# Folding q's shift row onto 64 partitions, and Wo with the masked sums split into high and low parts

## The chip, the cores and the metric

The kernel runs on one core of a Trainium2 chip. The metric is the device time of one execution in microseconds; the number for the kernel before is the median of three runs. Engines are named as in the profile: PE is TensorE's matmul stream (PEld its weight loads), DVE is VectorE, ACT is ScalarE, POOL is GpSimd, SP is SyncE, which only issues DMAs here.

## The reference

One block on a sequence of S = 2048 tokens with D = 448 channels, in float32. Six modulation rows of D numbers come from `silu(c) @ w_mod`. A linear-attention block and a token-mixing MLP follow, each with a layer norm, a scale and a shift ahead of it and a gate behind it:

```python
sa, ca, ga, sb, cb, gb = six rows of silu(c) @ w_mod
h = layernorm(x) * (1 + ca) + sa
q, k, v = split(h @ wqkv)              # 16 heads of 28
pq, pk = phi(q), phi(k)                # phi(t) = where(t > 0, t + 1, exp(t)) + 1e-6
kv = pk^T v per head;  z = sum of pk over the tokens
o = (pq kv) / (pq z + 1e-6)
x = x + ga * (o @ wo)
h = layernorm(x) * (1 + cb) + sb
x = x + gb * (gelu(h^T w1 + b1) w2 + b2)^T      # over the token axis, F = 1792
```

## The kernel before

The tokens are 16 tiles of 128. The order of the work is written out by hand: each engine does its instructions in the order in which the program text issues them, and what a helper issues lands at that place in the queues of all engines that it uses. A wait on one engine therefore holds up all that stands behind it there.

**Number formats.** A float32 matmul (`F32` operands) shows in the trace as two instructions, one of `F32R` operands as one. Most products are made as three `F32R` matmuls from a high and a low part of each operand. `split(full, hi, lo)` (line 82) makes the parts: a copy on ACT rounds to `hi`, a subtraction on DVE leaves `lo`.

**First stage: k, the sums and the first q.** The layer norm is folded into the projections. The scale `1 + ca` is multiplied into the weights (`w_high`, `w_low`); what the mean subtracts and what the shift `sa` adds come as a few extra rows of the moving operand, `Wrow[j]`, against matching rows of the tile of x (j = 0 for q, 1 for k). Those rows are made so: `row_part` (line 275) sums the raw weights times `sa` over the four chunks on DVE into `accb[j]`, 128 partitions by 448; `row_sum` (283) puts seven F32R matmuls with the selector `sel_s` into the bank `rowb[j]`; `row_bias` (289) ends the sum with one float32 matmul of `sel_b` and `accb[j]`; `row_out` (292) copies the rows into `Wrow[j]` with ACT and takes their low part with DVE. `close(t, j)` (437) is the last matmul of a projection and reads `Wrow[j]`.

The loop `for t in range(4, NT)` (682) issues, in each turn, the k projection of tile t+1 (`project`, line 684), `close(t, 1)`, at t=9 `row_sum(0)` and `row_bias(0)`, then the outer products of tile t-4 with its keys (`a_outer`, 545, into the four banks `cacc`), every second turn the transposition of statistics rows (`a_transpose`, 401), and from t=10 an early q projection (`a_q`, 476). The work of ACT and DVE comes after that in the text of the same turn: exponentials (`a_exp`), copies of the transposed rows (`a_copy`), splits of x (`a_split_high`, `a_split_low`), key parts (`a_pk_parts`, 517, the low part by an accumulating DMA from POOL's queue, line 528), the normed x and its parts (`a_norm`, `a_high`, `a_low`), at the end of t=9 `row_out(0)` (751), one step a turn of a modulation sum (`mod_part`, 227), and from t=13 Wo times the gate `ga` (779).

**Between the stages.** The last outer products, the key sum `zp`, two q projections, then `kvb` (818), the keys' products with v's weights in float32; `kvm` (822) is `kvb` times a mask that keeps the blocks of the heads. After one more q projection, four float32 matmuls (968) of `kvm` and the gated Wo make `wp`, 112 rows at a time; ACT copies them (970), DMAs lay them out in chunks of 128 rows (977), and `wp_split` (980) makes their high and low parts. `split_to` (319) splits pieces of w1 in the meantime, `load_to` loads them.

**Second stage.** For each tile a turn of the loop at 988: normalise the q side (`b_prod`, `b_sum`, `b_eps`, `b_recip`, `b_scale`), transpose, multiply by `wp`, add to x, second layer norm, and from turn 5 on the first product of the MLP. The rest of the MLP follows from line 1293 on, w2's products from 1319 on.

Of the kernel before, what the change touches and what calls it, by code (L numbers as in the profile page):

```python
# [8 lines left out]
F32 = mybir.dt.float32  # L9
# [5 lines left out]
P = 128  # L15
# [36 lines left out]
def block_kernel(ctx: ExitStack, tc: tile.TileContext, x, xt, wqkv, wo, w1, b1, w2, c, wmod, wfirst, out):  # L52
# [50 lines left out]
    cst.tile([P, 112], F32, name="space")  # L103
# [12 lines left out]
    sel_s = cst.tile([P, ROWS], F32R, name="sel_s")  # L116
    rowst = []
# [171 lines left out]
    def row_bias(j):  # L289
        nc.tensor.matmul(rowb[j][:ROWS, :D], sel_b, accb.pop(j), start=False, stop=True)  # L290
# [226 lines left out]
    def a_pk_parts(t):  # L517
        if t not in pks:
            a_pk_high(t)
        a_pk_low(t)  # L520
# [159 lines left out]
    wo_sb = []  # L680
    late = [t for t in range(NT) if t not in Q_EARLY.values()]
    for t in range(4, NT):
        if 5 < t < NT - 1:
            project(t + 1, 1, "kp")
        kp = close(t, 1) if t > 4 else kps[4]
        if t == 9:
            row_sum(0)
            row_bias(0)
# [28 lines left out]
        a_pk_parts(t - 1)  # L717
        highs = HIGH_AT.get(t, (t - 2,))
# [5 lines left out]
        if t == 11:  # L724
            low2 = mod_high(2)
# [24 lines left out]
        if t == 9:  # L750
            row_out(0)
# [8 lines left out]
        if t == 10:  # L760
            mod_add(2)
# [16 lines left out]
        if t >= 13:  # L778
            nc.vector.tensor_mul(wo_sb[t - 13], wo_sb[t - 13], mods[2][:G])
        load_to(PRE_LOAD.get(t, 0))  # L780


    a_pk_parts(NT - 1)
    nc.vector.tensor_add(pksum[1], pksum[1], pksum[0])
    zs = (moving(slot, "zh"), moving(slot, "zl"))
    split(pksum[1], *zs)
    load_to(10)
    a_phi_q()
    a_outer(NT - 4)
    a_outer(NT - 3)  # L790
    nc.vector.tensor_mul(wo_sb[3], wo_sb[3], mods[2][:G])
    for i in (2, 3):
        mod_part(3, i)
    split_to(2)
    a_outer(NT - 2)
    a_outer(NT - 1)
    zp = bank("zp")
    for i, pk in enumerate(zs):
        nc.tensor.matmul(zp[:, :D], ones_r, pk, start=(i == 0), stop=(i == 1))
    zb = tslot("zb")  # L800
    nc.scalar.activation(zb, zp[:, :D], AF.Copy, bias=S * 1e-6)
    load_to(14)
    split_to(4)
    a_q(late.pop(0))
    csum = []
    for ch in range(4):
        csum.append(slot(f"cs{ch}"))
        nc.scalar.activation(csum[ch], cacc[ch][:, :D], AF.Identity, scale=col[1][:, ch:ch + 1])
        nc.vector.scalar_tensor_tensor(csum[ch], zb, col[0][:, ch:ch + 1], csum[ch], op0=ALU.mult, op1=ALU.add)
    a_phi_q()  # L810
    a_q(late.pop(0))
    split_to(6)
    mp = mod_sum2(4)
    kvb = bank("kvb")
    for ch in range(4):
        for g in range(4):
            s = slice(g * G, (g + 1) * G)
            nc.tensor.matmul(kvb[:G, s], raw_w[2, ch][:, s], csum[ch][:, s], start=(ch == 0 and g == 0),  # L818
                             stop=(ch == 3), skip_group_check=True)
    a_phi_q()  # L820
    kvm = slot("kvm", parts=G)
    nc.vector.tensor_mul(kvm, kvb[:G, :D], mask)
    mod_out(4, mp)
    load_to(PRE + MID + 3)
    split_to(8)
    Wpr, Wph, Wpl = [], [], []


    H2h, H2l = [None] * NT, [None] * NT
    pns, phs, ys, opb, sums, nms, nm2s, rss, vss = {}, {}, {}, {}, {}, {}, {}, {}, {}  # L830

# [16 lines left out]
    def b_scale(t):  # L848
# [6 lines left out]
        pq[t] = None  # L855

# [106 lines left out]
    for fn in (b_prod, b_sum, b_eps, b_recip, b_scale):  # L963
        fn(0)
    mod_add(3)
    for g in range(4):
        wp = bank(f"wp{g}")
        nc.tensor.matmul(wp[:G, :D], kvm[:, g * G:(g + 1) * G], wo_sb[g], start=True, stop=True)  # L968
# [19 lines left out]
    for i in range(NT + LAG):  # L988
# [72 lines left out]
        if i == 0:  # L1061
            for ch in range(4):
                wp_split(ch)
# [323 lines left out]
```

## Time and profile before

| | |
|---|---|
| time, median of 3 runs (lowest to highest) | 433.37 us (433.33 to 433.41) |
| the profiled execution's own time | 434.09 us |
| its span, first to last instruction | 432.4 us |
| instructions | 7216 |
| DMA | 66.14 MB, mean 153 GB/s |

The page gives each engine's busy time in the whole span, then the chain of work that ended last, followed back from the end. The timelines list instructions with their start, their length and, in brackets, how long their engine stood idle before them and which instruction released it. A matmul's length there is that of one instruction from its start to its modelled end; matmuls overlap, so what one costs in a stream is the distance between the starts of two, or the length of a row of the chain over its count (`x11` is eleven instructions). The start of a row of the chain can be some tenths of a microsecond behind that of its first instruction in the timeline, since the chain gives the overlap to the earlier one. The table by windows gives, after the busy times, the granted clock, the busy share of the DMA engines (1 is full) and GB/s.

### The profile page before, as it was taken

What the parts mean: (1) busy time and instruction counts of PE and PEld (TensorE: products, weight loads), DVE (VectorE), ACT (ScalarE), POOL (GpSimd) and SP (SyncE); (2) the same over time, 40 slices, a digit from 0 to 9 for tenths busy, and PEclk for the clock granted to TensorE, in tenths of its full rate; (3) what the DMA queues carried; (4) which work ended last, traced back from release to release, by engine and by line L of the source; (5) the groups of instructions that cost most, each with busy time, mean ns of one, the idle gap of its engine ahead of it and who ended that gap; (6) DMA issues with size and microseconds to landing.
All of it is one profiled execution on the core that took longest, in us unless ns stands there. A gap on an engine that the chain in (4) does not pass through costs nothing.

```text
span 432.4 us, 7216 instructions
## 1 busy us (share of the span) xinstructions
PE 427.9 (99%) x2331; PEld 398.0 (92%) x2331; DVE 365.1 (84%) x814; ACT 278.9 (65%) x595; POOL 120.1 (28%) x199
## 2 busy tenths in 40 slices
PE   8999999999999999999999999999999999999997
PEld 8888899999899999999999999999999999999996
DVE  4899987889899999998579695739799998898894
ACT  5799869658578899996755263537464664655550
POOL 4345444300026577775200000010113131132010
PEclk9999999999999999999999999999999999999999
DMA  8997997565300036354427461577379977986431
GB/s 282 385 337 162 239 264 162 89 206 193 86 1 0 26 74 148 74 125 97 145 85 244 142 212 50 166 203 210 79 193 214 207 159 159 214 170 144 85 46 41
DMA packets 63797, 66.14 MB, mean 153 GB/s; under 512 B 4816, under 2 KB 55312, under 8 KB 63760
## 3 DMA queue, kind: packets, MB, share of 16 engines
q1 hardware_dynamic: 54688, 50.90, 37.8%
q0 software_dynamic: 8784, 14.32, 20.8%
q10 hardware_dynamic: 288, 0.46, 0.4%
q8 instruction: 18, 0.29, 0.3%
q14 instruction: 19, 0.16, 0.1%
HBM read 46.30 MB, written 7.34 MB: 124 GB/s over the span
## 4 chain that ended last, share of the span: by engine, by line
PE 97%; DVE 1%; ACT 1%; issue 0%
PE y L1183 19%; PE up L951 10%; PE up L950 10%; PE up L952 10%; PE y L1184 9%; PE cacc L554 7%; PE qp L432 7%; PE op L893 7%; PE kp L432 6%; PE op L900 1%; PE warm L188 1%; PE tq L863 1%; PE qp L439 1%; PE kvb L818 1%; PE wp L968 1%; PE rowb L287 1%
## 5 line engine op out<-in xcount | busy, mean ns | idle before, releaser
L950 PE MATMUL up<-h2h,ph 128*128 128x448 f32 x224 | 81.2, 362 | 0.0
L951 PE MATMUL up<-h2l,ph 128*128 128x448 f32 x224 | 81.2, 362 | 0.0
L952 PE MATMUL up<-h2h,pl 128*128 128x448 f32 x224 | 80.8, 361 | 0.0
L1138 POOL DMA_DIRECT2D a<-a x16 | 14.2, 964 | 142.6 <-DMA pr<-in_B_w_dram 76.7
L950 PEld LDWEIGHTS up<-h2h,ph 128*128 128x128 f32 x224 | 42.0, 188 | 3.1
L952 PEld LDWEIGHTS up<-h2h,pl 128*128 128x128 f32 x224 | 41.9, 187 | 3.0
L951 PEld LDWEIGHTS up<-h2l,ph 128*128 128x128 f32 x224 | 42.0, 188 | 2.3
L84 DVE TENSOR_TENSOR pl<-pr,ph 128x512 fp32r<-128x512 f32 x46 | 30.7, 688 | 2.6 <-ACT ph L83 1.7
L1189 ACT ACTIVATE cc<-y 128x448 f32<-128x448 f32 x24 | 13.0, 546 | 26.7 <-PE y L1184 26.7
L1102 DVE TENSOR_TENSOR u<-u,mod 128x448 f32<-128x448 f32 x14 | 8.7, 623 | 23.0 <-ACT u L1101 22.8
L83 ACT ACTIVATE ph<-pr 128x512 fp32r<-128x512 f32 x46 | 27.6, 623 | 0.8 <-PE up L952 0.5
L1101 ACT ACTIVATE u<-up,b 128x448 f32<-128x448 f32 x14 | 8.8, 625 | 25.4 <-PE up L952 24.9
L432 PE MATMUL kp<-wh,hh 128*128 128x448 f32 x64 | 23.8, 377 | 0.0
L554 PE MATMUL cacc<-pkh,xh 128*128 128x448 f32 x64 | 23.6, 369 | 0.0
L432 PE MATMUL qp<-wh,hh 128*128 128x448 f32 x64 | 23.5, 368 | 0.0
L1203 POOL DMA_DIRECT2D out_dram<-yt x14 | 12.7, 909 | 37.3 <-DVE yt L1194 27.9
L843 POOL TENSOR_SCALAR den<-den 128x16 f32<-128x16 f32 x16 | 8.8, 548 | 44.2 <-DVE den L840 44.2
L554 PE MATMUL cacc<-pkl,xh 128*128 128x448 f32 x56 | 20.3, 362 | 0.0
L893 PE MATMUL op<-wph,pth 128*128 128x448 f32 x48 | 18.7, 390 | 0.0
L1144 DVE TENSOR_TENSOR a<-a,s 128x512 f32<-128x512 f32 (+1 forms) x32 | 18.5, 622 | 0.0
L83 ACT ACTIVATE s2h<-s 128x512 fp32r<-128x512 f32 (+1 forms) x16 | 8.3, 569 | 15.5 <-DVE s L1144 15.5
L1183 PE MATMUL y<-ub,a11h 128*128 128x448 f32 x56 | 18.2, 375 | 0.0
(235 smaller groups left out, 1383.7 us busy)
## 6 DMA issues: line engine op xcount, KB each, us to landing
pr<-in_B_w_dram SPq DMA_DIRECT2D x56, 256.0 KB, 3.1
a<-in_B_w_dram SPq DMA_DIRECT2D x32, 256.0 KB, 4.8
a<-in_B_w_dram SPq DMA_DIRECT2D x32, 192.0 KB, 4.7
xt<-in_xt_dram SPq DMA_DIRECT2D x16, 256.0 KB, 5.0
x<-in_A_x_dram SPq DMA_DIRECT2D x16, 224.0 KB, 5.0
wm<-in_B_wmod_dram SPq DMA_DIRECT2D x16, 196.0 KB, 5.2
out_dram<-x SPq DMA_DIRECT2D x14, 224.0 KB, 2.3
out_dram<-yt POOLq DMA_DIRECT2D x14, 224.0 KB, 6.1
```

What stands on the lines that cost most here:

```text
L83: nc.scalar.activation(hi, full, AF.Copy)
L84: nc.vector.tensor_sub(lo, full, hi.bitcast(F32))
L432: nc.tensor.matmul(pps[t, j][:, :D], a[:, ch * P:(ch + 1) * P], w, start=first, stop=False)
L554: nc.tensor.matmul(cacc[ch][:, :D], a[:, s], b, start=(t == 0 and i == 0), stop=(t == NT - 1 and i == len(todo) - 1))
L893: nc.tensor.matmul(opb[t][:, :D], a, b, start=(ch == n == 0), stop=False)
L950: nc.tensor.matmul(ps[:, :D], hi[:, sl], mh, start=first, stop=False)
L951: nc.tensor.matmul(ps[:, :D], hi[:, sl], ml, start=False, stop=False)
L952: nc.tensor.matmul(ps[:, :D], lo[:, sl], mh, start=False, stop=last)
L1138: nc.gpsimd.dma_start(w, a, accum_op=ALU.add)
L1144: nc.vector.tensor_tensor(w, raw2[q, a][i], raw2[q, b][i], op=op)
L1183: nc.tensor.matmul(ps[:, :D], h[:, s], w, start=opens and r == 0, stop=False, skip_group_check=True)
L1184: nc.tensor.matmul(ps[:, :HD], l[:, s], wh, start=False, stop=closes and r == PAIRS - 1, skip_group_check=True)
```

## The change

Two products go from float32 to F32R.

*q's shift row.* The sum `accb[0]` on 128 partitions is folded onto 64 by an accumulating DMA from POOL's queue, issued at t=9 behind the key parts of tile 8. A new step `row_fold(0)`, at the end of t=9 where `row_out(0)` was, copies the selector to F32R (`sel_r`), writes the high part of the folded sum to partitions 0 to 63 of a new tile `both` and its low part to 64 to 127. `row_bias(0)` is then one F32R matmul. `row_sum(0)` and `row_bias(0)` move from behind `close(9, 1)` to the head of t=10, `row_out(0)` to behind `close(10, 1)`. `mod_add(2)` moves from t=10 to t=11.

*Wo.* `wo_split(g)` splits the gated Wo, two tiles at the end of t=14 and two behind `zb`. `kvm` is split too, and three F32R matmuls a tile take the place of one float32 matmul, in the order of the diff. To make room on ACT and DVE, the first tile's `b_prod` to `b_scale` move ahead of `kvm` or just behind it, and splits of w1 move back: six pieces instead of eight before the second stage, the other two between the `wp_split`s of its first turn.

```diff
-    cst.tile([P, 112], F32, name="space")
+    cst.tile([P, 14], F32, name="space")
...
+    sel_r = cst.tile([P, ROWS], F32R, name="sel_r")
...
     def row_bias(j):
-        nc.tensor.matmul(rowb[j][:ROWS, :D], sel_b, accb.pop(j), start=False, stop=True)
+        nc.tensor.matmul(rowb[j][:ROWS, :D], sel_r if j == 0 else sel_b, accb.pop(j), start=False, stop=True)
+
+    def row_fold(j):
+        acc, both = accb[j], moving(slot, f"rb{j}")
+        nc.scalar.activation(sel_r, sel_b, AF.Copy)
+        nc.scalar.activation(both[:64], acc[:64], AF.Copy)
+        nc.vector.tensor_sub(both[64:], acc[:64], both[:64].bitcast(F32))
+        accb[j] = both
...
+    def wo_split(g):
+        wos.append((moving(slot, f"woh{g}", parts=G), moving(slot, f"wol{g}", parts=G)))
+        split(wo_sb[g], *wos[g])
+
     late = [t for t in range(NT) if t not in Q_EARLY.values()]
     for t in range(4, NT):
+        if t == 10:
+            row_sum(0)
+            row_bias(0)
         if 5 < t < NT - 1:
             project(t + 1, 1, "kp")
         kp = close(t, 1) if t > 4 else kps[4]
-        if t == 9:
-            row_sum(0)
-            row_bias(0)
+        if t == 10:
+            row_out(0)
...
         a_pk_parts(t - 1)
+        if t == 9:
+            nc.gpsimd.dma_start(accb[0][:64], accb[0][64:], accum_op=ALU.add)
...
         if t == 11:
+            mod_add(2)
             low2 = mod_high(2)
...
         if t == 9:
-            row_out(0)
+            row_fold(0)
...
-        if t == 10:
-            mod_add(2)
...
+        if t == 14:
+            wo_split(0)
+            wo_split(1)
         load_to(PRE_LOAD.get(t, 0))
...
     nc.vector.tensor_add(pksum[1], pksum[1], pksum[0])
+    nc.vector.tensor_mul(wo_sb[3], wo_sb[3], mods[2][:G])
     zs = (moving(slot, "zh"), moving(slot, "zl"))
...
-    nc.vector.tensor_mul(wo_sb[3], wo_sb[3], mods[2][:G])
...
     load_to(14)
-    split_to(4)
+    wo_split(2)
+    wo_split(3)
     a_q(late.pop(0))
...
     a_q(late.pop(0))
-    split_to(6)
+    b_prod(0)
+    b_sum(0)
+    b_eps(0)
     mp = mod_sum2(4)
...
     a_phi_q()
+    b_recip(0)
+    mod_out(4, mp)
     kvm = slot("kvm", parts=G)
     nc.vector.tensor_mul(kvm, kvb[:G, :D], mask)
-    mod_out(4, mp)
+    b_scale(0)
+    kvh, kvl = slot("kvh", dt=F32R, parts=G), slot("kvl", dt=F32R, parts=G)
+    split(kvm, kvh, kvl)
     load_to(PRE + MID + 3)
-    split_to(8)
+    split_to(6)
...
     a_q(late.pop(0))
-    for fn in (b_prod, b_sum, b_eps, b_recip, b_scale):
-        fn(0)
     mod_add(3)
+    wps = [bank(f"wp{g}") for g in range(4)]
+    for gs in ((0, 1), (2,), (3,)):
+        for i, (a, b) in enumerate(((kvh, 0), (kvh, 1), (kvl, 0))):
+            for g in gs:
+                nc.tensor.matmul(wps[g][:G, :D], a[:, g * G:(g + 1) * G], wos[g][b], start=(i == 0), stop=(i == 2))
     for g in range(4):
-        wp = bank(f"wp{g}")
-        nc.tensor.matmul(wp[:G, :D], kvm[:, g * G:(g + 1) * G], wo_sb[g], start=True, stop=True)
+        wp = wps[g]
...
             for ch in range(4):
                 wp_split(ch)
+                split_to(max(6, 5 + ch))
```

85 lines of the change are left out of this document (43 added, 42 removed).

## The prediction

> **What bounds the kernel now.** I read the page's busy shares and chain first, then the list of what TensorE waited for.
>
> ```profile
> PE 427.9 (99%) x2331; PEld 398.0 (92%) x2331; DVE 365.1 (84%) x814; ACT 278.9 (65%) x595; POOL 120.1 (28%) x199
> PE 97%; DVE 1%; ACT 1%; issue 0%
> PE warm L188 <- DVE roots L108: 1.1, 1, 1.1
> PE rw L404 <- ACT rk L449: 0.2, 1, 0.2
> ```
>
> TensorE (PE) is busy from end to end, and 97% of the chain that ended last is its work. It waited twice in all, 1.3 us together: at the very start, and for `rw` at 27.6 (first row of the next fence). So a microsecond taken from its stream is a microsecond won, and a microsecond for which it is made to wait is one lost, with nothing later to swallow it. The second half decides here, because both parts of the change put new steps of other engines ahead of matmuls.
>
> The chain, in order of time, gives the two stretches that change (start, length):
>
> ```profile
> 27.59 0.29 PE rw L404
> 49.06 1.42 PE rowb L287 x7
> 50.48 0.75 PE rowb L290 x2
> 106.58 2.02 PE qp L432 x10
> 108.81 3.01 PE wp L968 x8
> ```
>
> **The gain.** An fp32 matmul shows as two instructions. The bias row (L290) costs 0.75 us in the stream, while the seven fp32r matmuls before it take 1.42, or 0.20 each. One fp32r matmul in its place saves 0.75 - 0.20 = 0.55 us. The Wo product (L968) is four fp32 matmuls in 3.01 us; twelve fp32r ones at 0.20 are 2.41 and save 0.60. That the stationary side is 98 or 112 columns wide makes no difference that these rows show: L287 has 98. Together 1.15 us. I see nothing that could make it larger; it could be some tenths smaller if the switches between the two formats cost the same as before.
>
> **The price of the fold.** The diff does the row sum at t=10, ahead of `project(11)`, and ends it with the matmul that reads `both`. That operand is made by `row_fold(0)`, whose two copies and one subtraction stand at the very end of t=9 on ACT and DVE, where `row_out(0)` stood. So the question is when TensorE reaches t=10, and when ACT and DVE reach the end of t=9. The timelines of the three engines and of GpSimd (POOL):
>
> ```profile
> 48.90 0.97 PE L287 MATMUL rowb<-wh,sel_s 128*98 128x448 f32 x4
> 50.72 0.71 PE L554 MATMUL cacc<-pkh,xh 128*128 128x448 f32 x1
> 53.29 0.27 PE L404 MATMUL rw<-ident,rowst 128*98 128x128 f32 x1
> 53.31 0.45 PE L432 MATMUL kp<-wh,hh 128*128 128x448 f32 x1
> ...
> 51.15 0.63 ACT L449 ACTIVATE rk<-kp,mv 128x448 f32<-128x448 f32 x1
> 53.59 0.57 ACT L407 ACTIVATE hl<-rw 34x128 fp32r<-34x128 f32 x2 [1.82 <-PE rw L404]
> 55.32 0.58 ACT L527 ACTIVATE pkl<-pkh 128x448 fp32r<-128x448 f32 x1
> 56.39 0.54 ACT L294 ACTIVATE wrow<-rowb 34x448 fp32r<-34x448 f32 x1
> ...
> 54.85 0.69 DVE L415 TENSOR_TENSOR hl<-xt,hh 128x512 fp32r<-128x512 f32 x1 [0.56 <-ACT hh L411]
> 56.40 0.23 DVE L505 TENSOR_TENSOR xh<-xn,xh 128x64 fp32r<-128x64 f32 x1 [0.32 <-ACT xh L500]
> 57.42 0.63 DVE L295 TENSOR_TENSOR wrow<-rowb,wrow 2x448 fp32r<-2x448 f32 x1
> ...
> 56.30 0.88 POOL L528 DMA_DIRECT2D pkl<-pk  x1 [3.45 <-ACT pkl L527]
> ```
>
> TensorE begins t=10 at 53.31, while DVE is at the end of t=9 only at 57.42 (L295, the old `row_out`): TensorE runs 4 us ahead. Before, that lead was harmless, since the finished row was not needed until `close(0, 0)`, late in t=10.
>
> TensorE, new: at 48.90 it goes straight to `a_outer(5)`, eleven matmuls at 0.20, then the transposition (to about 51.2), then the seven row matmuls, 1.4. It stands at the bias matmul at 52.7.
>
> ACT, new: the two `hl` copies no longer wait for the late transposition and start when `rk` ends, at 51.78 and not 53.59, 1.81 earlier. Everything behind them moves up: `pkl` ends at 55.32 + 0.58 - 1.81 = 54.1. POOL issues that low part's DMA (L528) 0.4 after `pkl` ends, as it did at 56.30, so at 54.5, and 0.88 later, at 55.4, it comes to the new DMA, which adds partitions 64 to 127 of `accb` to the others. The new DMA is behind L528 in POOL's queue, which is itself behind an ACT step.
>
> Its landing has these nearest rows: the first is the low-part DMAs between 44 and 64 us (224 KB, same queue), the second a plain DMA of the new one's size (112 KB) from SyncE's queue in a quiet stretch.
>
> ```profile
> DMA to landing us min/median/max: 4.4/5.0/6.3
> wpr<-wpg SPq DMA_DIRECT2D x2, 112.0 KB, 2.2
> 53.00:57.00 4.00, 4.00 (x22) 3.67 (x21) 3.09 (x8) 3.27 (x8) 0.70 (x1) 1.00 1.12 254
> ```
>
> The last row is the stretch 53 to 57 in the table by windows: the DMA engines' share is 1.12, they are full. So I take 4.1 us, close to the 4.4 of the same queue and place and a little less for half the bytes; bounds 2.2 and 6.3. It lands at 59.5. Then ACT's copy of 64 rows (0.55, as L294) and DVE's subtraction (0.63, as L295) end at 60.7, and TensorE goes on at 60.8: a wait of 8.1 us, from 6.2 to 10.3 by the bounds. ACT stands still behind that copy and DVE behind the subtraction; of what is queued there (`exp` of t=10, the next modulation product) TensorE needs nothing sooner, since it stands still too. Afterwards both are nearer to TensorE than before, and `row_out` has the whole of `project(11)` and `a_outer(6)` as cover.
>
> The Trainium skill (DMA: Bandwidth & Descriptors, Anatomy of one DMA) fits a GpSimd-issued DMA with 2.0 us plus the bytes over 436 GB/s: 2.3 us for this one, an estimate, and a wait of 6.3. By that fit the 224 KB DMAs would take 2.5, and here they took 4.4 to 6.3, so it does not describe this full stretch.
>
> **What the wait does to the clock.** TensorE has not stood still for long in this trace after its start, so the nearest rows are those of the start:
>
> ```profile
> 6.23 3.29 PE warm L188 x14
> 118.78 0.44 PE tq L863 x4
> 9.69 0.53 PE L432 MATMUL kp<-wh,hl 128*128 128x448 f32 x1
> 10.06 0.37 PE L432 MATMUL kp<-wl,hh 128*128 128x448 f32 x1
> 10.27 0.37 PE L432 MATMUL kp<-wh,hh 128*128 128x448 f32 x1
> ```
>
> A 128-column fp32 instruction took 0.235 us at the start and 0.11 later; the fp32r matmuls step from 0.37 to 0.21 us apart at 10.06. So out of rest TensorE runs at half rate for a while: the last unbroken run before the step lasts from 6.16 to 10.06, 3.9 us, and costs half of that. I take 2.0 us for the restart, with 0 (the rate does not fall) and 4.5 (half of all 9 us of the start) as bounds. The Trainium skill (TensorE: Matmul & The Clock Gate, HAM oscillation) says that an idle gap above one 3.4 us window halves the clock until a busy window has passed; by it the loss is 1.7 to 3.4 us, an estimate.
>
> **The price of the Wo split.** Four pairs of copy and subtraction are added, two of them at the end of t=14, with ACT's second copy behind DVE's product of the same tile:
>
> ```profile
> 87.28 0.62 ACT L465 ACTIVATE eq<-qp,mv 128x448 f32<-128x448 f32 x1
> 89.36 0.59 ACT L515 ACTIVATE pkh<-pk 128x448 fp32r<-128x448 f32 x1
> ...
> 88.58 0.62 DVE L779 TENSOR_TENSOR wo<-wo,mod 112x448 f32<-112x448 f32 x1
> 89.98 0.62 DVE L525 SCALAR_TENSOR_TENSOR pkl<-pk,pkh 128x448 fp32r<-128x448 f32 x1 [0.24 <-ACT pkh L515]
> 92.57 0.55 DVE L506 TENSOR_TENSOR xl<-xn,xh 128x384 fp32r<-128x384 f32 x1
> ...
> 94.26 0.36 PE L554 MATMUL cacc<-pkh,xl 128*128 128x448 f32 x1
> ```
>
> In old coordinates: ACT is free at 87.28, copies the first Wo tile, waits for the product of the second (88.58 + 0.55), copies it and reaches `eq` at 89.7, 2.4 later. `pkh` and with it DVE's `pkl` move to 92.4, and the subtractions behind them follow without a gap, so `xl` of tile 14 ends at 95.5 where it ended at 93.1. TensorE wants it at 94.26: a wait of 1.2, and some 0.1 more where `zl` is now behind the last Wo product. I take 1.3; bounds 0 and 2.4.
>
> At the Wo product the mask's product, two splits and `b_scale` lie in the cover of the q projection (2.02 us from 106.58): the high part is ready near 107.9, the low part near 108.5, and it is first read by the fifth matmul, 0.8 behind 108.7. I cost that at nothing; uncovered it would be 0.6. The moved `b_prod` to `b_scale` change places with w1 splits of the same length; `mod_add(2)`, 0.62 on DVE, has its reader many microseconds later; the copy of `sel_b` runs while ACT waits for the DMA.
>
> **Sum.** The profiled execution took 434.09 us, 0.72 above the median of 433.37. 434.09 - 1.15 + 8.1 + 2.0 + 1.3 = 444.3, and less 0.72: 443.6 us.
>
> **The rivals.** *The rate stays.* The wait of 8.1 comes, but TensorE resumes at full speed: 441.6. Against it stands the slow start; for it, that no later gap is in the trace.
> *DVE's queue alone decides.* If the new DMA lands by 56 us, the subtraction still waits for its turn: 57.42 less the two gaps of 0.56 and 0.32 is 56.5, done at 57.2, a wait of 4.5 us, perhaps too short to slow the clock: 434.09 - 1.15 + 4.5 + 1.3 - 0.72 = 438.0. Against it: no such DMA took under 4.4 in this stretch.
> *The lead is borrowed.* If TensorE had to wait later anyway for what ACT and DVE do in their own time, the waits would only come earlier, and the shorter stream would remain: 433.37 - 1.15 = 432.2, faster. That needs at least 9.4 us of later waits, and the list has none behind 28 us; or the fold's operand ready by 52.7, 8 us sooner than reckoned.
> *Longer still.* The DMA lands at the upper bound and the slow start is repeated whole: 434.09 - 1.15 + 10.3 + 4.5 + 1.3 - 0.72 = 448.3.
>
> **How the numbers follow.** 0.2%, or 0.9 us, is about what a measurement can tell from no change. Forecast 0.50, the rate stays 0.20, DVE alone 0.14, longer 0.09, borrowed lead 0.06, something that cancels to within 0.2% 0.01. That makes slower 0.93, same 0.01, faster 0.06. The range from 438.0 to 446.5 leaves out the borrowed lead, the lower half of DVE alone and most of the longest case; the forecast's own range is 441.7 to 445.5.
>
> **What would show it.** In the profile after: a wait of TensorE of about 8 us before the bias matmul, released by DVE's subtraction, with ACT's copy waiting for the new DMA; fp32r matmuls 0.37 us apart behind it for some 4 us; a wait of about 1 us in the outer products of tile 14 at `xl`; twelve Wo matmuls in 2.4 us. If TensorE waits under 2 us at the bias matmul, I have misjudged its lead, and the forecast is wrong as a whole.

## The result and the profile after

| | before | changed |
|---|---|---|
| time, median of 5 runs each (lowest to highest) | 433.41 us (433.33 to 433.42) | 448.44 us (446.54 to 448.76) |
| ratio, with its 95% interval | | 1.0337 [1.0316, 1.0359] |
| the profiled execution: time, span | 434.09, 432.4 us | 448.5, 446.8 us |

The change costs 15.0 us by the medians, where 10.2 were forecast. The ratio, here and below, is that of the means, so it can differ a little from that of the medians. The page of the changed kernel, its busy shares and its chain by engine:

```profile
PE 432.5 (97%) x2334; PEld 399.6 (89%) x2334; DVE 368.6 (83%) x820; ACT 282.1 (63%) x602; POOL 122.0 (27%) x200
PE 83%; DVE 9%; ACT 3%; DMA 2%; issue 1%; POOL 1%; SPq 0%; ACTq 0%
```

TensorE is busy for 97% of the span and no longer 99%, and only 83% of the chain is its own: steps of VectorE, ScalarE, a DMA and GpSimd now stand in it. The list of what TensorE waited for:

```profile
PE rowb L291 <- DVE rb L297: 8.8, 1, 8.8
PE cacc L562 <- ACT xh L508: 0.6, 1, 0.6
PE cacc L562 <- DVE xl L514: 0.3, 1, 0.3
```

The first is the wait for the folded row, the next two are the one at tile 14. The chain of the changed kernel shows what the first is made of (start, length):

```profile
55.23 0.54 POOL pkl L536
55.77 5.01 DMA accb<-accb
60.80 0.58 ACT rb L296
61.41 0.63 DVE rb L297
62.09 0.69 PE rowb L291
62.78 3.19 PE kp L440 x10
72.90 2.21 PE cacc L562 x11
75.22 2.05 PE qp L440 x10
```

The step that GpSimd has to issue first, the DMA, the copy, the subtraction, the matmul: one behind the other, and 5.01 of it is the DMA. Then ten projection matmuls take 3.19 us where ten take 2.05 later. The timeline and the table by windows (the stretch 62 to 66, its third number from the end being the granted clock) say why:

```profile
62.57 0.57 PE L440 MATMUL kp<-wh,hh 128*128 128x448 f32 x1
62.95 0.57 PE L440 MATMUL kp<-wl,hh 128*128 128x448 f32 x1
...
65.19 0.37 PE L440 MATMUL kp<-wl,hh 128*128 128x448 f32 x1
```

```profile
62.00:66.00 4.00, 3.92 (x12) 3.52 (x13) 1.94 (x5) 0.54 (x1) 0.00 (x0) 0.60 0.65 172
```

The matmuls stand 0.37 us apart from 62.57 to 65.19 and 0.20 from there, and the bias matmul ahead of them, started at 62.09, is slow too, since the next one starts 0.48 behind it. The granted clock of those four microseconds is 0.60, against 1.00 in the stretch of before that the prediction quoted (53 to 57). The Wo product, by the timeline of the changed kernel:

```profile
121.11 0.57 PE L995 MATMUL wp<-woh,kvh 112*112 112x448 f32 x2
121.51 0.57 PE L995 MATMUL wp<-wol,kvh 112*112 112x448 f32 x2
...
122.94 0.36 PE L995 MATMUL wp<-woh,kvh 112*112 112x448 f32 x1
```

Ten of the twelve take from 121.11 to 123.1, so all of them 2.4 us, as forecast.

Where the other microseconds are shows only when the same instruction is looked up in both traces and its two starts are compared. The differences, after less before, at points of the kernel before's time:

| at (us of before) | difference | what lies between this row and the one above |
|---|---|---|
| 26 | +0.43 | the first k projections |
| 54.4 | +10.04 | the wait for the row, less the bias matmul's gain, and the first slow matmuls |
| 56 | +10.40 | the rest of the slow clock |
| 85 | +10.73 | no wait at all |
| 106 | +12.41 | tile 14, with the two waits, 0.9 together |
| 112 | +11.89 | the Wo product, 0.52 won |
| 127 | +12.23 | first turn of the second stage, no wait |
| 139 | +13.12 | turns two to five, a listed wait of 0.2 |
| 212 | +13.95 | no wait |
| 296 | +13.94 | the MLP's first product alone |
| end | +14.4 | the MLP's second product, no wait |

Two things here were not in the prediction: a drift in stretches without any wait (0.43, 0.33, 0.34, 0.83, 0.46: about 2.4 us together), and a loss of 0.9 in turns two to five of the second stage. Some 0.3 of the 0.9 would be drift as well, an estimate from the stretch before it (0.34 in 15 us). The drift has a plain sign in the chains. First of before, then of the changed kernel:

```profile
9.52 6.32 PE kp L432 x30
...
69.17 2.22 PE cacc L554 x11
71.39 2.00 PE qp L432 x10
```

```profile
9.52 6.68 PE kp L440 x30
```

Ten q matmuls take 2.05 instead of 2.00 (their row stands above), or 2.5% more. Thirty k matmuls take 6.68 instead of 6.32, which is more than that; in the run with the pool put back (below) 0.19 of the 0.43 at 26 us remain, so a part of this first stretch is not the drift. Outer products do not drift: eleven take 2.21 here and 2.22 before. The kp and qp matmuls stream weights from the pool `tok`; outer products stream key parts from another pool. And between the two kernels `tok` has moved: `space` is 98 columns smaller and `sel_r`, rounded up, takes 32 bytes more than that, so that all that lies behind them is 32 bytes higher (`wh0` at 203424 instead of 203392 in the built program).

The theory after this: the price of 15 us is four things, namely the row's wait with its slow clock, the wait at tile 14, new waits in the first turns of the second stage, and 2.5% on each matmul whose streamed operand lies 32 bytes off. Rivals: that the drift is part of the clock, and that the loss in the second stage only follows from the earlier waits.

### The profile page after: what moved, and what is told of

It reads as the page before. It is cut to its first block, busy times and chain, and to the rows that moved or that the text cites. A ratio compares the mean times of both kernels' runs of the same rounds, so it can differ in the third digit from the quotient of the medians.

```text
span 446.8 us, 7237 instructions
## 1 busy us (share of the span) xinstructions
PE 432.5 (97%) x2334; PEld 399.6 (89%) x2334; DVE 368.6 (83%) x820; ACT 282.1 (63%) x602; POOL 122.0 (27%) x200
## 4 chain that ended last, share of the span: by engine, by line
PE 83%; DVE 9%; ACT 3%; DMA 2%; issue 1%; POOL 1%; SPq 0%; ACTq 0%
PE y L1213 18%; PE up L977 10%; PE up L979 10%; PE up L978 10%; PE y L1214 9%; PE op L920 6%; PE qp L440 5%; PE kp L440 4%; PE cacc L562 4%; PE warm L189 1%; PE op L927 1%; PE tq L890 1%; DMA accb<-accb 1%; DVE st L388 1%; DVE hl L423 1%
## 5 line engine op out<-in xcount | busy, mean ns | idle before, releaser
L1213 PE MATMUL y<-ub,a12h 128*128 128x448 f32 x56 | 18.2, 374 | 0.0
```

What stands on the lines that cost most here:

```text
L1213: nc.tensor.matmul(ps[:, :D], h[:, s], w, start=opens and r == 0, stop=False, skip_group_check=True)
```

## The experiments

Totals below are medians, with the ratio's interval, against the kernel before in the same set of runs (433.4 to 433.8 us). The start of a program differs from one execution to the next: some traces begin their first k projection at 6.9 to 7.8 us and not at 9.17, and lead by up to 0.8 us before any changed instruction. So traces are compared by the steps in their difference, not by its absolute value.

### The two halves alone

The row part alone, with `space` of 6 columns so that nothing behind moves:

```diff
-    cst.tile([P, 112], F32, name="space")
+    cst.tile([P, 6], F32, name="space")
+    sel_r = cst.tile([P, ROWS], F32R, name="sel_r")
...  the row part of the change, nothing of Wo
```

> The kernel before with the fold of q's shift row alone, as in the change, and the pool at its old address. Theory A (TensorE waits at the bias matmul for the fold, then runs slowly for some microseconds): the start of the next projection is 9.26 us later in the changed kernel, 0.48 of it from before t=9, and 1.1 are lost behind it to the slow rate: 433.4 + 8.8 + 1.1 = 443.3. Rival: part of the 15 us of the change is made by both parts together, and this one gives much less, or much more.

443.97 us, 1.0236 [1.0219, 1.0253], near the theory's 443.3. The wait at the bias matmul is 9.0, and from 76 us of before to the end the difference in the traces stays at +10.7 within 0.03: no drift, no later loss. So the fold with its clock costs about 10.5, and the row part costs nothing anywhere else. The rival about the second stage falls here: a wait of 9 us alone brings no loss there. The slow stretch, though, is twice as long in this execution. TensorE's timeline, the first and the last of the slow matmuls:

```profile
61.12 0.69 PE L291 MATMUL rowb<-rb,sel_r 128*98 128x448 f32 x1 [9.01 <-DVE rb L297]
...
67.20 0.38 PE L562 MATMUL cacc<-pkl,xh 128*128 128x448 f32 x1
```

From 61.12 to 67.20 it runs at half rate, 6.1 us, where the changed kernel's lasts 3.1 (62.09 to 65.19) after nearly the same wait. By the distances of the matmuls that costs 2.9 us here and some 1.4 there. So the length of the wait does not fix the price of the restart.

The Wo part alone, at the kernel before's addresses (the change with its row part and `space` taken back):

> The kernel before with the Wo part alone, as in the change, and the pool at its old address. From the trace of the changed kernel: 1.4 us lost in the outer products of tile 14, 0.57 won in the twelve matmuls: 433.4 + 0.85 = 434.3. Rival: the Wo part also costs in the loop behind it, where the changed kernel loses another microsecond between its first output matmul and the first product of the MLP: 435.4.

437.40 us, 1.0087 [1.007, 1.0103]: both figures too low. TensorE's two longest waits that this kernel adds:

```profile
PE op L915 <- DVE pth L900: 1.4, 1, 1.4
PE cacc L554 <- ACT xh L500: 0.7, 1, 0.7
```

The step at tile 14 is +1.64, the product gives 0.55 back, and then 2.9 us go in the first turns of the second stage. The timeline there (ScalarE and SyncE's DMAs):

```profile
109.81 2.18 ACT L83 ACTIVATE ph<-pr 128x512 fp32r<-128x512 f32 x4
111.90 1.82 ACT L987 ACTIVATE wpg<-wp 112x448 f32<-112x448 f32 x4
112.45 5.07 SPq L994 DMA_DIRECT2D wpr<-wpg  x8
121.01 0.58 ACT L83 ACTIVATE wph<-wpr 128x448 fp32r<-128x448 f32 x1 [1.88 <-DMA wpr<-wpg]
```

and the same in the kernel before:

```profile
109.60 0.55 ACT L970 ACTIVATE wpg<-wp 112x448 f32<-112x448 f32 x1 [2.45 <-PE wp L968]
110.17 5.12 SPq L977 DMA_DIRECT2D wpr<-wpg  x8
117.05 0.58 ACT L83 ACTIVATE wph<-wpr 128x448 fp32r<-128x448 f32 x1 [0.66 <-DMA wpr<-wpg]
```

Before, ScalarE stands ready when the product comes and copies its first part at once. Now four pieces of w1 (2.18 us) stand ahead of those copies in its queue, and SyncE's eight layout DMAs begin 2.28 later, of which 1.64 are TensorE's own lag. More pieces of w1 stand between the copies of what they bring. The last of these copies is at 121.01 instead of 117.05, and the `pth` copies of the next tile, for which TensorE waits, are behind it. But the order of the queues explains only a part of those 4 us. The layout DMAs' times to landing, at most 2.6 us before, are here:

```profile
DMA to landing us min/median/max: 2.0/2.3/4.0
```

The last one, 112 KB, takes 4.0 us, though the DMA engines are busy for only 3% of its last two microseconds (the second last number, for the last of them):

```profile
120.00:121.00 1.00, 1.00 (x8) 0.94 (x7) 0.00 (x0) 0.00 (x0) 0.00 (x0) 1.00 0.03 4
```

Such a late landing stands in the profiled execution of four of the eleven kernels that have the Wo part (this one, the next, and two below) and of none of the nine without it; the changed kernel's own profile does not have it. Each kernel has one trace, so it is not seen to come and go within one, but this profiled execution is the slowest of its four runs (437.00 to 438.05). So the first turns are judged by medians from here on, not by one trace.

### The addresses

The changed kernel with `space` of 6 columns instead of 14:

> The changed kernel with one number changed: the unused tile `space` is 6 columns wide and not 14, so that the second tile pool (`tok`, which holds the split weights of the projections and of Wo) starts at the same address as before; in the changed kernel it starts 32 bytes higher. Theory A: matmuls whose moving operand lies in that pool take 0.205 us and not 0.200 for the 32 bytes (528 projection and output matmuls, and 14 of the row sums, by 0.0052), so 2.8 us come back: 445.6. Rival B: the 2.5% come from something else that the change does (other traffic, the clock): 448.4, as the changed kernel.

446.55 us (446.39 to 448.54), 1.0307 [1.0281, 1.0332]: 1.9 of the 2.8 come back. Its profiled execution is the slowest of the four, with the late landing (4.2) and 3.0 us lost between 121 and 136 us, against 1.0 in the changed kernel; but it has no drift: the difference is +14.47 to +14.48 from 139 us to the end.

The kernel before, with nothing changed but the filler:

```diff
-    cst.tile([P, 112], F32, name="space")
+    cst.tile([P, 120], F32, name="space")
```

> The kernel before with `space` 120 columns wide and not 112, so that the same pool starts 32 bytes higher; nothing else is changed. Theory A: the same matmuls at 0.205 us, 433.4 + 2.8 = 436.2. Rival B: 433.4, the address of a tile has no price.

436.02 us, 1.0055 [1.004, 1.007]: 2.5 us for 32 bytes, without one instruction changed and with no new wait. Chain of this kernel:

```profile
70.87 2.05 PE qp L432 x10
```

Its difference grows by 2.5 us from 26 us to the end, in the same stretches as in the changed kernel. This settles the drift against the clock. What it does not tell is whether the streamed operand's own address counts, or that of anything else in the pool. So the kernel before with its buffers in place and only the operands shifted inside them, 32 bytes to the left, 64 to the left, 64 to the right:

```diff
     def moving(new, name, dt=F32R, parts=P):
-        return new(name, dt=dt, parts=parts, w=512)[:, 16:16 + D]
+        return new(name, dt=dt, parts=parts, w=512)[:, 8:8 + D]
```

(`0:D` in the second, `32:32 + D` in the third.)

> Kernel before, with one edit: every operand that the kernel lays out for TensorE to stream (weights of q, k and v, phi of k, the modulation halves, Wo's product, hidden activations) starts 32 bytes further left in its buffer, so at 32 past a multiple of 64 bytes; the buffers themselves stay. Theory (a streamed operand at 32 past a multiple of 64 costs 0.205 instead of 0.200 us for 448 columns): about 168 cacc, 672 up, 144 op and 350 kp and qp matmuls, 1334 x 0.005 = 6.7 us, 440.1 us, and the spacing in the up matmuls 0.205. Rival (it was the place of the pool, or of what ScalarE, VectorE and DMA touch): 433.4 us, at most 434.

438.65 us, 1.0118 [1.0105, 1.0131], a good 5 us: less than 6.7, but of the theory's size, and the outer products are slow now too. Chain:

```profile
71.29 2.07 PE qp L432 x10
...
76.06 2.27 PE cacc L554 x11
```

> As the run before, 64 bytes to the left instead of 32: every streamed operand starts at the head of its buffer, again at a multiple of 64. Theory (the unit is 64 bytes): 433.4 us, ratio 1.000. Rival (a larger unit, 128 bytes or more, or the neighbour buffers count): 436 us or more.

437.01 us, 1.0078 [1.0065, 1.0091]. The theory misses, since it is no unit of 64 bytes, and the rival's 436 or more holds. Ten q matmuls take 2.03, between 2.00 and 2.07:

```profile
71.56 2.03 PE qp L432 x10
```

> Kernel before, with every streamed operand 64 bytes further right in its buffer (128 bytes from its head instead of 64). Theory (what counts is the start address within 128 bytes: 64 is the quick one, 0 costs half of the extra, 32 and 96 all of it): as with 64 to the left, 437.0 us, ratio 1.008. Rival (distance to the buffer's head or to the neighbours counts): 433.4 us.

437.87 us, 1.0094 [1.008, 1.0108]: like 64 to the left or a little worse, and not as before.

```profile
71.00 2.04 PE qp L432 x10
```

With buffers that start at multiples of 128 bytes, the start 64 bytes behind such a multiple is the only quick one of those tried (0.200 us); 0 behind it costs 0.203 to 0.204 and 32 or 96 behind it 0.204 to 0.207. That the two places at 0 differ from each other (the difference grows by 2.9 us from 26 us to the end in one, 4.3 in the other) says that a period of 128 is not the whole rule; what the rest is stays open.

### What sets the wait for the row

The row part alone, with VectorE's addition at the DMA's place:

```diff
-            nc.gpsimd.dma_start(accb[0][:64], accb[0][64:], accum_op=ALU.add)
+            nc.vector.tensor_add(accb[0][:64], accb[0][:64], accb[0][64:])
```

> The row part alone, with the fold added by DVE at the place where the change issues its DMA; the order is otherwise that of the change. Theory A (the queues of DVE and ACT at the end of t=9 set the wait, the DMA only lengthens it): DVE comes to the fold's subtraction at about 57.8 and ends it at 58.4, TensorE stands at the bias matmul from about 52.7, so it waits 5.8 us and not 9; with the slow rate behind it (about 1.1 us lost) the time is 444.0 - 3.3 = 440.7. Rival (the DMA alone is the cost): without it the wait is gone and the time is 433.4 - 0.55 = 432.9.

440.11 us, 1.0162 [1.0147, 1.0177]. The wait shrinks from 9.0 to 5.0 and does not vanish; the queues of t=9 alone are worth 5: VectorE works there without a pause from 46.8 us until it has made `rb` at 57.4. And the clock falls behind this shorter wait too. Timeline, and the window 58 to 62, with a granted clock of 0.66:

```profile
57.50 0.69 PE L291 MATMUL rowb<-rb,sel_r 128*98 128x448 f32 x1 [4.96 <-DVE rb L297]
57.99 0.58 PE L440 MATMUL kp<-wh,hh 128*128 128x448 f32 x1
```

```profile
58.00:62.00 4.00, 4.00 (x15) 3.64 (x14) 1.38 (x4) 0.81 (x2) 1.22 (x2) 0.66 0.86 210
```

Next, the addition in t=8 behind `row_part(0, 3)`, `row_fold(0)` at the head of ScalarE's and VectorE's t=9, and the row sum in t=10 behind `close(10, 1)`, 2.2 us later for TensorE:

```diff
             row_part(0, t - 5)
+            if t == 8:
+                nc.vector.tensor_add(accb[0][:64], accb[0][:64], accb[0][64:])
```

> The row part alone with the fold taken out of the path: DVE adds the halves of accb at t=8, right behind the last row_part; the copies and the subtraction stand at the head of t=9's work on ACT and DVE; the row sum stands behind close(10). Theory A: both is ready near 53.5, TensorE needs it near 54.9, so no wait is left and the matmul's gain of 0.55 us shows: 432.9. Rival (moving the row sum behind t=9 costs by itself, because row_out then comes late for close(0, 0)): a wait of 1 us or more there, 434 or above.

433.57 us against 433.39, 1.0004 [0.9995, 1.0013]. The wait is gone, and so is all of the 10.5; the gain of 0.55 does not show in the total either. Yet it is won: the bias matmul, 0.75 us in the chain of before, takes 0.20 in this one. Chain, VectorE's timeline, then TensorE's:

```profile
55.37 0.20 PE rowb L291
...
49.37 0.62 DVE L717 TENSOR_TENSOR accb<-accb 64x448 f32<-64x448 f32 x1
...
51.06 0.16 DVE L406 TENSOR_TENSOR rowst<-mv,rowst 128x4 fp32r<-128x4 f32 x1
...
51.28 0.32 PE L412 MATMUL rw<-ident,rowst 128*98 128x128 f32 x1 [0.32 <-DVE rowst L406]
```

The added 0.62 us pushes `rowst` back, and the transposition waits for it; with the first matmuls behind it, that costs as much as the bias matmul gains. So the addition was moved behind the two `rowst` operations:

> Row part alone as in the early version, but VectorE's add behind the two rowst operations of t = 8 instead of ahead of them. Theory (the row transposition waited for rowst, 0.5 us): no wait there, 432.9 us, ratio 0.9988. Rival (the pass is late for something else then, xl or hl): 433.3 us or more, with a wait at a close or at the outer product.

433.96 us against 433.82, 1.0004 [0.9995, 1.0013]: the rival. The wait for `rowst` is gone and one for `hl`, the next operation in VectorE's queue, has come:

```profile
50.27 0.62 DVE L744 TENSOR_TENSOR accb<-accb 64x448 f32<-64x448 f32 x1
50.99 0.69 DVE L423 TENSOR_TENSOR hl<-xt,hh 128x512 fp32r<-128x512 f32 x1
51.73 0.47 PE L440 MATMUL kp<-wh,hl 128*128 128x448 f32 x1 [0.46 <-DVE hl L423]
```

### What the splits of Wo and w1 cost

Gate products one turn earlier (`t >= 12`) and the splits of Wo's tiles 0 and 1 in t=13 and t=14, behind `a_pk_parts`:

> The Wo part alone, with the four products with the gate one turn earlier (t=12 to 15) and the first two splits behind the key parts at t=13 and t=14, so that ACT doesn't wait for a product. Theory A: the 1.4 to 1.6 us at the outer products of tile 14 go, and the loss in the first turns of the second stage stays: 437.4 - 1.5 = 435.9. Rival: that loss is only the first one handed on, then 434.

440.32 us, 1.0164 [1.0148, 1.018]: my place was worse than the change's. Timeline:

```profile
81.08 0.56 ACT L83 ACTIVATE woh<-wo 112x448 fp32r<-112x448 f32 x1
81.67 0.62 DVE L84 TENSOR_TENSOR wol<-wo,woh 112x448 fp32r<-112x448 f32 x1 [5.61 <-ACT woh L83]
```

VectorE stands for 5.61 us at the subtraction of Wo, because the copy is in ScalarE's queue behind copies that wait for a transposition. What VectorE makes for the outer products is late for two tiles; TensorE waits for them four times, 3.1 us in all, and its granted clock from 92 to 102 us is 0.84. By 101 us the difference is +5.8.

The same, with w1's pieces spread: 2 and 3 ahead of the `wp_split`s, 4 to 7 one a turn in the turns after, their low parts by GpSimd's accumulating DMAs, and no piece of w1 between `kvm` and the copies of the product:

```diff
-    split_to(6)
...
+            split_to(4)
             for ch in range(4):
                 wp_split(ch)
-                split_to(max(6, 5 + ch))
...
-        split_to(8 + max(0, i - 5))
+        split_to(min(8, 4 + i) + max(0, i - 5))
```

> As the run before, and no w1 piece is split between kvb and the copies of wp, nor behind the wp_splits: pieces 2 and 3 ahead of the wp_splits of the first turn, pieces 4 to 7 one a turn behind it and their low parts by DMA from POOL's queue; the twelve matmuls tile by tile. Theory A: the loss of the first turns comes from the w1 splits that stand on ACT ahead of the copies of wp, and so ahead of the eight layout DMAs (0.58 us of issue each, one behind the other on SP), and from the splits that stand on DVE behind the wait for the last of them; without these it goes, and the gain of 0.57 shows: 432.9. Rival (the moved work itself is too much for DVE, wherever it stands): 434 or more.

440.01 us, 1.0138 [1.0117, 1.016]: the early loss stays (+5.7 at 101), as its place was not changed. From 112 to 148 us the difference only goes from +5.12 to +5.16, and the wait for `pth` is gone. By the medians, though, the two kernels are 0.3 apart. The profiled execution of the one before has the late landing and this one has not, so the traces of this pair do not tell what the spread is worth. The runs on record tell more, when they are sorted by the granted clock of the whole execution. At 0.996 the kernel before took 440.70 and 441.45 us and this one 439.85 to 440.29; at 0.999 to 1.0 it took 439.63 and 439.93, and this one 437.89 and 438.03. So the spread is worth some 1 to 2 us, and the slow stretch near 100 us does not come in every execution.

Now the early loss too: the splits of tiles 0 and 1 where w1's pieces 0 and 1 were split, those two behind the second late q tile.

```diff
         mod_part(3, i)
-    split_to(2)
+    wo_split(0)
+    wo_split(1)
```

> Only the Wo part, with other places for its work: each gate product one turn earlier, the splits of all four pieces of Wo between the last turns of stage one and the mask (0 and 1 where w1's pieces 0 and 1 were split, 2 and 3 as in the change), w1's pieces 0 and 1 split after the second late q tile, 2 and 3 just ahead of the splits of the product, 4 to 7 one a turn, and the twelve matmuls tile by tile. Theory (the loss of the Wo part, 3.9 us + 0.55 us of gain unseen, is the wait for a gate product at tile 14 and the w1 splits ahead of the layout copies): no wait of TensorE above 0.2 us between the tile 14 and the fourth turn of the second stage, 432.9 us, ratio 0.999. Rival (eight more ScalarE and VectorE passes find no room there wherever they stand): 436 us or more, with TensorE waiting for xl, pth or pn.

434.17 us against 433.49, 1.0019 [1.0007, 1.003], between the theory and the rival. Of the Wo part's 3.9 us 3.2 are gone, by the medians: the 1.64 at tile 14, and as much again in the first turns, for which the changed places of w1's pieces remain as the reason. Left are two things: the product gains nothing, and the step of 0.6 between 148 and 157 us, in the eighth turn. The product begins 0.2 late, and its third matmul, which reads the low part of `kvm` (ready at 109.6), starts 0.36 behind the second. The order tile by tile costs nothing as such: in the run before, where TensorE comes to it 5.7 later, the same order takes 2.4 us (114.35 to 116.77). Three runs on that. The matmuls in the change's order and two pieces of w1 a turn; then this order and one piece a turn; then this without GpSimd:

> The Wo part as in the run with late splits, but the twelve matmuls in the change's order (tiles 0 and 1 together) and w1's pieces 4 to 7 two a turn, in turns one and two. Theory (the gain of 0.57 us was lost because the tiles one by one stand for the reloaded weights, and 0.6 us were lost at turn eight because GpSimd's queue, with one piece a turn, was late with the small sums): 432.9 us, ratio 0.9988, the twelve matmuls in 2.4 us, no step at turn eight. Rival (the losses are from the added passes as such): 433.8 to 434.4.

435.29 us, 1.0032 [1.0021, 1.0043]. The twelve take 2.5 us; no step at turn eight; but 2.5 us are lost from 120 to 136 us, with waits for `pth` and `pn` and, in this execution, the late landing. The rival's price is exceeded.

> The Wo part with late splits, one w1 piece a turn as there, but the twelve matmuls in the change's order. Theory (tiles one by one cost the 0.3 to 0.6 us that the order gains, and nothing else of that run changes): the step of 0.6 us at turn eight stays, 433.8 us. Rival (an earlier Wo product brings the waits of the next turns back): 434.5 us or more.

434.02 us against 433.74, 1.0011 [1.0002, 1.002], near the theory. The step at turn eight is there (0.5). The product gains 0.24, not 0.55: TensorE comes to it at 108.17 by the difference of the traces and starts at 108.39, and the first pair stands 0.5 apart from the second instead of 0.4. TensorE waits for the high part of `kvm`, which ScalarE copies until 108.34; ahead of that in the chain stand the mask's product and the first tile's `b_prod` to `b_recip`, which the change moved there. I had costed all this at nothing since it lay under the q projection. With TensorE 1.6 us late, as in the change, it does; with TensorE in time it does not.

> As the run before, but the low parts of w1's pieces 4 to 7 by VectorE instead of GpSimd's DMAs. Theory (the step at turn eight comes from GpSimd's queue, which is late with the small sums): no step there, 433.2 us. Rival (VectorE is full in those turns, 19.25 of 20 us from 126 to 146 us, so that four more passes of 0.69 us come out on TensorE): 434.5 us or more, with TensorE waiting for pn or pth in turns two to five.

435.96 us, 1.006 [1.0042, 1.0077]: the rival again. The step at turn eight is smaller (0.15), but the same four passes on VectorE cost 2.4 us between 128 and 140:

```profile
133.98 0.44 PE L912 MATMUL op<-wph,pth 128*128 128x448 f32 x1 [0.87 <-DVE pth L897]
```

### Both halves, mended

The Wo part with late splits and VectorE's addition at the end of t=8:

> The Wo part of the run before with the row part as a VectorE add at the end of t = 8, the fold at the head of t = 9, the row sum behind the close of tile 10, and space of 6 columns, so that nothing moves. Theory (both gains, 0.55 and 0.57 us, are real once nothing waits): 432.3 us, ratio 0.9975, no wait for rowst. Rival (each new pass on VectorE or ScalarE makes some operand as much later as TensorE gains): 433.2 to 434.0, with a wait of 0.3 us or more at the row transposition or behind it.

435.48 us, 1.005 [1.0035, 1.0064], more than the rival's price. Here ScalarE stands at the copy of the folded row, and with it `hl`:

```profile
53.37 0.58 ACT L296 ACTIVATE rb<-accb 64x448 fp32r<-64x448 f32 x1 [2.39 <-DVE accb L793]
...
55.33 0.48 PE L447 MATMUL kp<-wrow,hl 98*128 98x448 f32 x1 [1.87 <-ACT hl L415]
```

The row part with the addition behind `rowst`, and the Wo part with two pieces a turn:

> The two runs before together, everything at the kernel before's addresses. Theory: the gains add, 0.55 + 0.57, 432.3 us, ratio 0.9974. Rival (they share a cover on VectorE and ScalarE): 432.9 us or more.

434.58 us against 433.82, 1.0018 [1.0009, 1.0027]: the rival. No version that I found beats the kernel before. The table by windows of the kernel before suggests why (stretch, length, then busy time of PE, PEld, DVE, ACT, POOL):

```profile
44.00:56.00 12.00, 12.00 (x60) 10.61 (x59) 11.30 (x28) 10.04 (x21) 4.81 (x5) 1.00 1.10 239
92.00:106.00 14.00, 14.00 (x86) 13.27 (x85) 13.12 (x26) 10.04 (x21) 0.00 (x0) 1.00 0.67 218
126.00:146.00 20.00, 20.00 (x107) 18.58 (x107) 19.25 (x46) 14.40 (x36) 11.24 (x21) 1.00 0.02 3
```

VectorE is busy for 94%, 94% and 96% of the three stretches into which the new passes go. The page's 84% is an average over the whole span. TensorE sets the time there with VectorE right behind it: the passes of 0.6 to 0.7 us added to VectorE in the first and the third stretch came out on TensorE as waits of 0.3 to 0.9, and of 1.9 where ScalarE stood for the result, in each place that was tried; the gains were 0.55 and 0.55. For the third stretch two runs show that the engine is the reason, since the same four passes cost 1.9 us more on VectorE than by way of GpSimd (435.96 against 434.02). For the other two it is argued from the waits and not tested by taking work off VectorE.

## Why the prediction was wrong

The direction, the main mechanism and its place were right, and the terms that the prediction has were near. It was 4.8 us too low (448.44 against 443.6). By the differences of the two traces: 2.4 for the missing drift (some 0.2 of it the start's), 0.9 for turns two to five, which were costed at nothing (some 0.3 of it drift too), 0.4 more than forecast for the row with its clock (10.40, less a drift of 0.48 until then, is 9.9, for 8.1 + 2.0 - 0.55), 0.4 more at tile 14, 0.1 less gained at the Wo product, and 0.7 because the profiled run of after, 448.5, lies at its median and not 0.7 above it, as that of before did.

- *The gain.* Right at the Wo product, 0.52 to 0.59 for 0.60 in all kernels where TensorE reached it late. Right at the bias row too, 0.75 against 0.20 in the chains; with no long wait left it was eaten by what VectorE's pass delayed.
- *The fold.* Forecast 8.1, measured 8.8 of idle time. The steps came as written: the low part's DMA issued at 55.23 (54.5 forecast), the new one at 55.77 (55.4), landing after 5.0 (4.1), two steps behind it. The landing was the mis-sized term, by 0.9; it belonged with the DMAs of its queue and stretch, whose median is 5.0, and half the bytes did not make it shorter. By the Trainium skill's fit for a GpSimd DMA (DMA: Bandwidth & Descriptors, Anatomy of one DMA) the estimate for it was 2.3 us; the measurement differs, and decides.
- *The slow restart.* Forecast 2.0, measured 1.1 between 53.3 and 55.6 us of before (+9.26 to +10.40), where seven matmuls stand 0.37 apart, and 0.3 more in the slow bias matmul ahead of them: 1.4 together, in a slow stretch of 3.1 us. In the row part alone it was 2.9, in one of 6.1 us. So the 2.0 lies between two executions' losses, and that it came near both is luck: the start of the program, a slow stretch of 3.9 us, could not tell how much this differs. The Trainium skill (TensorE: Matmul & The Clock Gate, HAM oscillation) names idle gaps above about 3.4 us as those after which the clock is halved. The waits of 5.0 and 8.8 us here agree; the four of at most 1.5 us, with a granted clock of 0.84, show that shorter ones can do it too. Of the two losses, 1.4 lies below the prediction's estimate by that rule, 1.7 to 3.4, and 2.9 within it.
- *Tile 14.* Forecast 1.3; measured 0.9 of waits and 1.7 of difference from 85 to 106 us. Near enough, and the reason as written, `eq` and `pkh` behind the copies of Wo; but the longer wait, 0.6, is for `xh` from ScalarE, and only 0.3 for `xl`, which the forecast named.
- *The missing term.* The diff's line on `space` was in front of me, 112 columns becoming 14, with `sel_r` beside it. I took it for bookkeeping. It moves a pool by 32 bytes, and that alone costs 2.5 us (the kernel before with 120 columns). This is the largest term that was left out. With the pool put back the changed kernel takes 446.55, at the upper end of the range and still 3.0 above the forecast, so it is not the only one.
- *The step costed at nothing.* "The moved `b_prod` to `b_scale` change places with w1 splits of the same length" is true of VectorE's total and false of the order. The splits of w1 that had stood ahead of `kvm` now stood, four in a row, between `kvm` and ScalarE's copies of the product, and ahead of a chain that runs through eight DMAs of SyncE, four copies and four subtractions to the next tile's `pth`. I had followed the moved operations to their readers, but not what stands behind them on their engine. In the change this is worth 0.9, in the Wo part alone some 1.6 (its 3.9 less the 1.64 at tile 14 and the 0.7 that remained with the pieces elsewhere).

The parts measured alone come to more than the whole: row +10.5, Wo +3.9, addresses +2.5 are 16.9, and the change costs 15.0. That slower matmuls leave ScalarE and VectorE more time in the first turns would make such a difference, and so would the late landing, which the change's executions need not have had; the runs do not tell the two apart.

Of the rivals, *longer still* had the right size (448.3) for the wrong reasons: neither bound that it adds, the landing of 6.3 and the slow start of 4.5, was seen. *The rate stays* fell with the granted clock of 0.60, *DVE's queue alone* with the DMA, which landed at 60.8. With VectorE's addition in the DMA's place its wait of 4.5 was near (5.0), but that one was not too short to slow the clock (0.66). *The borrowed lead* fell as well. With the row's operand in time there was no debt of 9 us waiting later; the kernel simply came back to its old time.

What stays open: what makes the last layout DMA land up to 2 us late in some executions; what sets the length of the slow stretch behind a wait; why 64 bytes to either side do not cost the same, and whether the step at turn eight in the runs with GpSimd's four extra DMAs is only its queue (without them the step shrank to 0.15, but those four passes then cost TensorE other waits ahead of that turn).

## What to carry to other kernels

A gain of half a microsecond on the bound engine was not won here by adding a pass to an engine that is 95% busy in the same stretch; read the busy shares by stretch, not over the span, before you look for a place. When an operation moves, list what stands behind it in its queue at the new place and follow that to the next reader on the bound engine, through DMAs too. And when a diff changes the size of a constant tile, look where the pools behind it come to lie: compare the spacing of unchanged matmuls in both traces first, since a drift without a wait is not a matter of the order of work.

## What the runs showed of the hardware that was not expected

- The place of a streamed F32R operand counts. For 448 columns, a start 64 bytes behind a multiple of 128 gave 0.200 us a matmul, a start at such a multiple 0.203 to 0.204, one 32 or 96 behind it 0.204 to 0.207; moving operands by 32 bytes cost the whole kernel 2.5 us (one pool) and 5.2 us (all operands made by `moving`).
- TensorE's rate can fall after waits far shorter than 9 us: after one of 5.0 us the granted clock was 0.66 for the next four microseconds, and with four waits of at most 1.5 us, 3.1 in all, it was 0.84 from 92 to 102 us, while a single wait of 1.9 us (the first run with both halves) left it at 1.00 from 52 to 60 us. The slow matmuls are 0.37 us apart in all cases.
- The slow stretch behind a wait has no fixed length: 3.1 us after a wait of 8.8 us, 6.1 us after one of 9.0.
- A plain DMA of 112 KB landed after 2.2 to 2.3 us in sixteen profiled executions and after 3.5 to 4.2 in four, with the DMA engines busy for 3% of the last 2 us of it in three of these and 10% in the fourth.
- A DMA of 112 KB that adds into the same tile took 5.0 us (5.3 and 4.7 in two other kernels) in a stretch in which the DMA engines were full for the most part, as long as the median of those of 224 KB in the same queue.
